# The joint network's first chunk: its tanh rows by DMA transposes instead of TensorE, and an earlier place for the next chunk's x tiles

## The chip, the cores and the metric

The kernel runs on one core of a Trainium2 chip. The metric is the device time of one execution in microseconds; lower is better. The engines are named as in the profile: PE (TensorE, with PEld for its weight loads), DVE (VectorE), ACT (ScalarE), POOL (GpSimd) and SP (SyncE), which here only issues DMAs.

## The reference, cut to what matters

The kernel computes the forward and the backward pass of a small transducer ("joint") network in bfloat16:

```python
B, T, D, K, U = 2, 16000, 256, 3, 8
h  = gelu(conv3(x, w1))[:, ::2]            # (B, 8000, D)
f  = gelu(conv3(h, w2))[:, ::2]            # (B, 4000, D)
fe = f @ w_f                               # (B, 4000, D)
ge = g @ w_g                               # (B, U, D)
j  = tanh(fe[:, :, None] + ge[:, None])    # (B, 4000, U, D)
out = j @ w_o                              # (B, 4000, U, D)
# and the gradients of x, w1, w2, g, w_f, w_g, w_o for a given grad_out
```

Two matmuls read j with different sides on the partitions. `out` takes j as it is made (D on partitions, time along the row). The gradient of w_o is the sum over time of j times grad_out, so it needs j with time on the partitions: the "tanh rows".

## The kernel before, in words

**Tiling.** The 4000 time steps of each of the two sequences are cut into 8 chunks of 512 (the last has 416), so there are G = 16 chunks, n = 0 to 15. In a chunk the 8 values of u are taken in 4 pairs, `up` = 0 to 3.

**Main work of a pair** (`joint_units`, L602): for each of its two u, `gj` (L518) makes the square of tanh JSQ on ACT (L523), multiplies GOT (grad_out, transposed as it is loaded) with w_o on PE (L529) and forms NGZ on DVE (L531); POOL adds NGZ up (L550). Then `o_block` (L618) makes four blocks of the output, 128 time steps each: four matmuls JT x WO (L623), an eviction on ACT (L625), and one store for the pair (L652). Between these blocks stand the matmuls of `gwo` (L664, L672), which add the tanh rows JR times GO (grad_out in natural layout) of the pair before into the PSUM bank GWO_ps. Ahead of the output blocks, `ahead()` (L800) starts the tanh of the next pair (L312, ACT, into JT) and calls `load_jr` (L552) for it.

**Tanh rows.** `load_jr` takes a JR tile (3 buffers). In chunks 1 to 15 it fills it with four DMA transposes on SP's queue (L563), one for each of two u and two halves of D, 128 x 512 each, from JT. In chunk 0 it returns at L558 with the tile empty, and `joint_units` calls `jr_block` (L597) for each of the four blocks: four PE transposes into a PSUM tile (L380) and one copy of 128 x 512 by DVE (L382).

**Fill.** While the pairs of chunk n run, PE also makes the two convolutions and FE of chunk n + 1 (`conv_units` L246, `conv2_units` L279, `fe_units` L302, gelu on ACT and DVE at L197 and L199) and, from n = 1 on, the backward convolutions of chunk n - 1. `weave` (L681) takes `ratio` units of this fill for each unit of the main work. Chunk 1's first tanh needs chunk 1's FE.

**Queues and order.** The program's text does not fix the order on an engine: a scheduler places the instructions when the kernel is built, each engine then runs its own list strictly in order, and tiles from small pools (x tiles XC: 6 buffers, GOT: 6, GO: 3, PSUM tiles: 7) are waited for when they come free. SP's queue carries the loads of XC (L134, L138; transposing), GOT (L144; transposing), GO (L152) and the JR transposes (L563). Before the first chunk, L749 to L755 load GOT for u = 0 and 1, GO of pair 0, GOT for u = 2 and 3, and then the four x tiles of chunk 1. In each pair, one x tile of chunk n + 2, one GO and two GOT are loaded (L790 to L798).

Of the kernel before, what the change touches and what calls it, by code (L numbers as in the profile page):

```python
# [32 lines left out]
def kernel(  # L33
# [27 lines left out]
    G = len(chunks)  # L61
    xq = x.rearrange("b (q four) d -> b four q d", four=4)

    def geom(n):
        b, ci = chunks[n]
        c0 = ci * CW
        return b, ci, c0, min(CW, MQ - c0)

    def blocks(w):
        return [(o, min(P, w - o)) for o in range(0, w, P)]  # L70
# [59 lines left out]
    def load_x(n, c):  # L130
        b, ci, c0, W = geom(n)
        t = xcp.tile([P, KT, CW + 16], BF16, name="XC")
        if c == 3 and ci > 0:
            nc.sync.dma_start_transpose(out=t[:, :, 0:W + 16], in_=xq[b, c, c0 - 16:c0 + W, :])  # L134
        else:
            if c == 3:
                nc.vector.memset(t[:, :, 0:16], 0.0)
            nc.sync.dma_start_transpose(out=t[:, :, 16:16 + W], in_=xq[b, c, c0:c0 + W, :])  # L138
        S[n]["X", c] = t

    def load_got(n, u):
        b, ci, c0, W = geom(n)
        t = gotp.tile([P, KT, CW], BF16, name="GOT")
        nc.sync.dma_start_transpose(out=t[:, :, 0:W], in_=grad_out[b, c0:c0 + W, u, :])  # L144
        S[n]["GOT", u] = t

    def load_go(n, up):
        b, ci, c0, W = geom(n)
        t = gop.tile([P, 4, 2 * V], BF16, name="GO")
        nfull = W // P  # L150
        src = grad_out[b, c0:c0 + nfull * P, 2 * up:2 * up + 2, :]
        nc.sync.dma_start(out=t[:, 0:nfull, :], in_=src.rearrange("(tb p) u v -> p tb (u v)", p=P))  # L152
        S[n]["GO", up] = t
        r = W - nfull * P
        if r and up % 2 == 0:
            t = tailp.tile([P, V], BF16, name="GOs")
            for i in range(4):
                nc.sync.dma_start(out=t[i * r:(i + 1) * r, :], in_=grad_out[b, c0 + nfull * P:c0 + W, 2 * up + i, :])
            S[n]["GOs", up // 2] = t
# [358 lines left out]
    def gj(n, u):  # L518
        b, ci, c0, W = geom(n)
        st = S[n]  # L520
        JT, GOT = st["JT", u], st["GOT", u]
        JSQ = jsp.tile([P, KT, CW], BF16, name="JSQ")
        nc.scalar.activation(out=JSQ[:, :, :W], in_=JT[:, :, :W], func=ACT.Square)  # L523
        NGZ = ngzp.tile([P, KT, CW], BF16, name="NGZ")
        st["NGZ", u] = NGZ
        for mt in range(KT):
            ps = ps_f32()
            for kt in range(KT):
                nc.tensor.matmul(ps[:, :W], lhsT=WOT[:, kt, mt * P:(mt + 1) * P], rhs=GOT[:, kt, :W],  # L529
                                 start=(kt == 0), stop=(kt == KT - 1))  # L530
            nc.vector.scalar_tensor_tensor(out=NGZ[:, mt, :W], in0=JSQ[:, mt, :W], scalar=1.0, in1=ps[:, :W],  # L531
                                           op0=ALU.subtract, op1=ALU.mult,
                                           accum_out=NGGEc[:, b, mt, u, ci:ci + 1])
            yield
# [17 lines left out]
    def load_jr(n, up):  # L552

        W = geom(n)[3]
        nfull = W // P
        JR = jrp.tile([P, 4, 2, KT, P], BF16, name="JR")
        S[n]["JR", up] = JR
        if n == 0:  # L558
            return
        for j in range(2):  # L560
            JT = S[n]["JT", 2 * up + j]
            for kt in range(KT):
                nc.sync.dma_start_transpose(out=JR[:, 0:nfull, j, kt, :], in_=JT[:, kt, 0:nfull * P])  # L563
# [38 lines left out]
    def joint_units(n, up, ahead):  # L602
        b, ci, c0, W = geom(n)
        st = S[n]
        bl = blocks(W)[:W // P]
        us = (2 * up, 2 * up + 1)
        for u in us:
            yield from gj(n, u)
            ngfe_acc(n, u)
            short_jt(n, u)  # L610
        if n == 0:
            for k in range(len(bl)):
                jr_block(n, up, k)
                yield
        OUT = outp.tile([P, 4, 2 * V], BF16, name="OUT")
        JR = st["JR", up]

        def o_block(k):  # L618
            o, M = bl[k]
            ps = ps_f32()  # L620
            for j, u in enumerate(us):
                for kt in range(KT):
                    nc.tensor.matmul(ps[:M, j * V:(j + 1) * V], lhsT=st["JT", u][:, kt, o:o + M], rhs=WO[:, kt, :],  # L623
                                     start=(kt == 0), stop=(kt == KT - 1))
            nc.scalar.copy(out=OUT[:M, k, :], in_=ps[:M, :])  # L625

        ahead()
        pend = prev_gwo[0]
        o_block(0)
        yield  # L630
        o_block(1)
        yield
        if pend is not None:
            gwo(*pend, 0)
        yield
        if pend is not None:
            gwo(*pend, 1)
        yield
        for k in range(2, len(bl)):
            o_block(k)  # L640
            yield
            if pend is not None:
                gwo(*pend, k)
        yield
        if pend is not None:
            gwo_rest(*pend, len(bl))
        yield
        if W % P and up % 2:
            yield from short_block(n, up // 2)
        prev_gwo[0] = (n, up)  # L650
        nfull = W // P
        nc.gpsimd.dma_start(out=out_0[b, c0:c0 + nfull * P, us[0]:us[1] + 1, :].rearrange("(tb p) u v -> p tb (u v)", p=P),  # L652
                            in_=OUT[:, 0:nfull, :])
# [94 lines left out]

    for i in range(2):  # L749
        load_got(*order[i])  # L750
    load_go(*orderp[0])
    for i in range(2, 4):
        load_got(*order[i])
    for c in (1, 0, 3, 2):
        load_x(1, c)  # L755
    for _ in chain(warm(16), small_units(), conv_units(0), transposed_units(), warm(4), conv2_units(0), warm(16), fe_units(0)):
        pass
    for u in range(2):
# [3 lines left out]
    for n in range(G):  # L762
        back, fwd = n > 0, n + 1 < G
        conv = conv_units(n + 1) if fwd else iter(())
        parts = []
        if back:
            for (o, M) in blocks(window(n - 1)[1] - window(n - 1)[0]):
                load_x5(n - 1, o, M)
            d1, e, gwf = d1_units(n - 1), e_units(n - 1), gwf_units(n - 1)
            nfn = (len(blocks(geom(n - 1)[3])) + 1) // 2  # L770
            d5, gw2 = d5_units(n - 1), gw2_units(n - 1)
            nhg = len(blocks(geom(n - 1)[3]))
            parts += [islice(conv, 2), islice(d1, 1), islice(conv, 1), d1, conv,
                      islice(gwf, 1), islice(d5, 1), islice(gwf, nfn - 1), islice(d5, 1), islice(gw2, 1),
                      islice(d5, 1), islice(gw2, 1), d5, islice(gw2, nhg - 2), gwf, gw2]
        else:
            parts += [conv, iter([None] * 3)]
        if fwd:
            parts.append(conv2_units(n + 1))
        if back:  # L780
            parts.append(islice(e, 6))
        else:
            parts.append(iter([None] * 3))
        if fwd:
            parts.append(fe_units(n + 1))
        if back:
            parts.append(e)
        fill = chain(*parts)
        ratio = (0.85 if n > 0 else 0.28) if n + 1 < G else 0.72
        for up in range(U // 2):  # L790
            step = n * (U // 2) + up
            if n + 2 < G:
                load_x(n + 2, (1, 0, 3, 2)[up])
            if step + 1 < len(orderp):
                load_go(*orderp[step + 1])
            for i in range(2):
                if 2 * step + 4 + i < len(order):
                    load_got(*order[2 * step + 4 + i])  # L798

            def ahead():  # L800
                for i in range(2):
                    if 2 * step + 2 + i < len(order):
                        tanh(*order[2 * step + 2 + i])
                if step + 1 < len(orderp):
                    load_jr(*orderp[step + 1])

            weave(joint_units(n, up, ahead), fill, ratio)
            if up == U // 2 - 1:
                for _ in fill:
                    pump(2)  # L810
                pump(len(later) + len(lazy))
                lazy_on[0] = False
    n = G - 1
# [44 lines left out]
    t_ = gel3.tile([P, 512], BF16, name="g_sq", tag="g_sq")  # L858
    nc.scalar.activation(out=t_[:], in_=GWG_ps[:], func=ACT.Copy, scale=-1.0)
    nc.sync.dma_start(out=out_6.rearrange("(dt p) n -> p dt n", p=P), in_=t_[:].rearrange("p (k n) -> p k n", k=KT))  # L860


# [1 line left out]
_INS = ['x', 'w1', 'w2', 'g', 'w_f', 'w_g', 'w_o', 'grad_out']  # L864
_OUTS = [((2, 4000, 8, 256), 'bfloat16'), ((2, 16000, 256), 'bfloat16'), ((3, 256, 256), 'bfloat16'), ((3, 256, 256), 'bfloat16'), ((2, 8, 256), 'bfloat16'), ((256, 256), 'bfloat16'), ((256, 256), 'bfloat16'), ((256, 256), 'bfloat16')]
# [25 lines left out]
```

## Time and profile before

| | us |
|---|---|
| median of the 3 runs | 872.27 |
| the three runs | 867.04, 872.27, 877.83 |
| the profiled execution | 865.23 |
| its span in the profile | 863.5 |
| PE, DVE, ACT, POOL busy in it | 830.8, 603.8, 685.7, 410.6 |
| DMA queue q1 (SP), share of 16 engines | 76.4% |

The span is counted from the first to the last thing that the profile holds; the time of the execution has 1.7 us more around it. All times in a trace are counted from the span's start. In the rows of a timeline, the first number is the start, the second the length, "x16" joins that many equal instructions, and the bracket tells how long the engine sat idle before and what ended that. A group row gives busy time and mean length in ns. For SP, a row is the time in which the queue issued the DMA, not that of the transfer.

### The profile page before, as it was taken

Reading aid. Unit: us, or ns where it says so; the run is one execution under the profiler, and the core shown is the slowest. Engines: PE = TensorE matmul, PEld = TensorE weight load, DVE = VectorE, ACT = ScalarE, POOL = GpSimd, SP = SyncE. Lnnn points to the kernel's source line nnn. Section 1 sums busy time; section 2 is a strip of 40 time slices with the busy share of each in tenths; the row PEclk is TensorE's granted clock in tenths of the full one; section 3 lists DMA queues with packets and bytes.
Section 4 is the critical chain, followed back from the end, with each engine's and each line's share of the span. In section 5 each row is a group of like instructions: output and inputs, shape, how many; then the busy total and the mean of one; then the engine's idle time right before and its main releaser. Section 6 shows DMA issues by size and latency. Waiting matters only on the chain.

```text
span 863.5 us, 17775 instructions
## 1 busy us (share of the span) xinstructions
PE 830.8 (96%) x6648; PEld 598.9 (69%) x6648; DVE 603.8 (70%) x1194; ACT 685.7 (79%) x1067; POOL 410.6 (48%) x457
## 2 busy tenths in 40 slices
PE   8878999999999999999999999999999999999997
PEld 4455776767777677777766677776766867777875
DVE  4797949669495784949578495875949579495553
ACT  4889896986969869696996969788696986969534
POOL 1264553544544544555454455453554544455651
PEclk9999999999999999999999999999999999999999
DMA  9998999999999999999899999999999999999942
GB/s 187 211 215 195 189 250 224 224 243 193 258 206 227 226 217 233 212 227 219 211 203 214 234 215 240 227 210 250 177 263 236 205 211 219 219 243 219 215 140 91
DMA packets 382455, 185.66 MB, mean 215 GB/s; under 512 B 330160, under 2 KB 366280, under 8 KB 382368
## 3 DMA queue, kind: packets, MB, share of 16 engines
q1 hardware_dynamic: 362400, 114.35, 76.4%
q0 software_dynamic: 19968, 70.18, 27.9%
q8 instruction: 52, 0.85, 0.4%
q14 instruction: 35, 0.29, 0.1%
HBM read 54.43 MB, written 50.34 MB: 121 GB/s over the span
## 4 chain that ended last, share of the span: by engine, by line
PE 51%; DVE 30%; ACT 13%; issue 3%; DMA 2%; POOL 0%; ACTq 0%; POOLq 0%; DVEq 0%
PE ps L500 7%; PE ps L246 7%; PE GWO_ps L672 7%; PE ps L529 7%; PE ps L478 7%; PE ps L623 6%; DVE NGZ L531 6%; DVE G L199 5%; DVE g_sq L199 5%; DVE g_s L197 5%; DVE GH L369 3%; ACT JSQ L523 3%; ACT JT L312 3%; PE pst L380 3%; PE ps L366 3%
## 5 line engine op out<-in xcount | busy, mean ns | idle before, releaser
L550 POOL TENSOR_TENSOR ACCN<-ACCN,NGZ 128x1024 f32<-128x1024 f32 (+1 forms) x80 | 170.4, 2130 | 126.5 <-DVE NGZ L531 124.0
L531 DVE SCALAR_TENSOR_TENSOR NGZ<-JSQ,ps 128x512 bf16<-128x512 bf16 (+1 forms) x256 | 163.4, 669 | 83.5 <-ACT GX L481 47.7
L523 ACT ACTIVATE JSQ<-JT 128x1024 bf16<-128x1024 bf16 (+1 forms) x128 | 135.3, 1060 | 86.6 <-DVE NGZ L531 86.6
L312 ACT ACTIVATE JT<-FE,GE 128x512 bf16<-128x512 f32 (+1 forms) x256 | 171.0, 736 | 0.1
L625 ACT CAST OUT<-ps 128x512 bf16<-128x512 f32 x248 | 147.7, 614 | 3.8 <-PE ps L623 3.3
L623 PE MATMUL ps<-WO,JT 128*128 128x256 bf16 x992 | 148.1, 272 | 0.9 <-DVE NGZ L531 0.5
L529 PE MATMUL ps<-GOT,WOT 128*128 128x512 bf16 (+1 forms) x512 | 138.4, 374 | 1.7 <-DVE JR L382 1.1
L672 PE MATMUL GWO_ps<-GO,JR 128*128 128x256 bf16 x992 | 139.7, 273 | 0.0
L197 DVE SCALAR_TENSOR_TENSOR g_s<-g_sq,g_x 128x1024 bf16<-128x1024 bf16 (+1 forms) x45 | 74.6, 1657 | 57.1 <-ACT g_sq L197 57.1
L623 PEld LDWEIGHTS <-JT 128*128 128x128 bf16 x992 | 94.4, 98 | 24.9 <-issue 1.4
L672 PEld LDWEIGHTS <-JR 128*128 128x128 bf16 x992 | 95.1, 98 | 18.2 <-issue 1.1
L322 DVE TENSOR_TENSOR ACC<-ACC,ps 128x512 f32<-128x512 f32 x90 | 59.4, 682 | 66.6 <-PE ps L500 62.0
L478 PE MATMUL ps<-W1T,GH 128*128 128x256 bf16 (+2 forms) x768 | 104.2, 273 | 0.0
L500 PE MATMUL ps<-rows,X 128*128 128x256 bf16 (+2 forms) x768 | 94.2, 272 | 8.2 <-DVE rows L382 8.2
L246 PE MATMUL ps<-XC,W 128*128 128x512 bf16 (+1 forms) x384 | 91.1, 374 | 2.5 <-DMA XC<-in_x_dram 2.1
L500 PEld LDWEIGHTS <-X 128*128 128x128 bf16 (+2 forms) x768 | 74.5, 98 | 23.1 <-issue 11.5
L652 POOL DMA_DIRECT2D out_dram<-OUT x64 | 49.6, 775 | 85.2 <-ACT OUT L625 82.8
L481 ACT CAST GX<-ps 128x512 bf16<-128x512 f32 (+2 forms) x128 | 74.4, 592 | 15.0 <-PE ps L478 7.8
L478 PEld LDWEIGHTS <-GH 128*128 128x128 bf16 (+2 forms) x768 | 75.0, 99 | 15.6 <-issue 1.7
L529 PEld LDWEIGHTS <-WOT 128*128 128x128 bf16 x512 | 49.1, 98 | 43.9 <-issue 2.6
L490 POOL DMA_DIRECT2D out_dram<-GX x64 | 35.9, 560 | 87.3 <-ACT GX L481 81.0
L382 ACT COPY rows<-pst 128x1024 bf16<-128x1024 bf16 x64 | 63.0, 1018 | 9.6 <-PE pst L380 9.5
(139 smaller groups left out, 1264.5 us busy)
## 6 DMA issues: line engine op xcount, KB each, us to landing
GO<-in_grad_out_dram SPq DMA_DIRECT2D x56, 512.0 KB, 5.3
out_dram<-OUT POOLq DMA_DIRECT2D x56, 512.0 KB, 5.6
X<-in_x_dram POOLq DMA_DIRECT2D x58, 320.0 KB, 8.0
out_dram<-GX POOLq DMA_DIRECT2D x58, 256.0 KB, 4.1
JR<-JT SPq DMA_TRANSPOSE x240, 5.1
GO<-in_grad_out_dram SPq DMA_DIRECT2D x8, 384.0 KB, 4.1
out_dram<-OUT POOLq DMA_DIRECT2D x8, 384.0 KB, 4.7
GOT<-in_grad_out_dram SPq DMA_TRANSPOSE x128, 4.6
```

The source lines that it names most:

```text
L197: later.popleft()()
L246: nc.tensor.matmul(ps[:, :W], lhsT=W1[:, i, kt, mt * P:(mt + 1) * P], rhs=st["X", c][:, kt, 16 + sh:16 + sh + W], start=(k == 0), stop=(k ...
L312: nc.scalar.activation(out=JT[:, mt, :W], in_=S[n]["FE"][:, mt, :W], func=ACT.Tanh, bias=GE[:, b, mt, u:u + 1], scale=1.0)
L478: nc.tensor.matmul(ps[:Mx, cj * D:(cj + 1) * D], lhsT=GH[:, par, kt, j:j + Mx], rhs=W1T[:, i, kt, :], start=(k == 0), stop=(k == last))
L500: nc.tensor.matmul(ps[:, dt * D:(dt + 1) * D], lhsT=st["X5", o][:M, i + 2 * par, dt * P:(dt + 1) * P], rhs=t[:M, j + 2 * par:j + 2 * par + ...
L523: nc.scalar.activation(out=JSQ[:, :, :W], in_=JT[:, :, :W], func=ACT.Square)
L529: nc.tensor.matmul(ps[:, :W], lhsT=WOT[:, kt, mt * P:(mt + 1) * P], rhs=GOT[:, kt, :W], start=(kt == 0), stop=(kt == KT - 1))
L531: nc.vector.scalar_tensor_tensor(out=NGZ[:, mt, :W], in0=JSQ[:, mt, :W], scalar=1.0, in1=ps[:, :W], op0=ALU.subtract, op1=ALU.mult, accum_ ...
L550: nc.gpsimd.tensor_tensor(out=out, in0=in0, in1=st["NGZ", u][:, :, :W], op=ALU.add)
L623: nc.tensor.matmul(ps[:M, j * V:(j + 1) * V], lhsT=st["JT", u][:, kt, o:o + M], rhs=WO[:, kt, :], start=(kt == 0), stop=(kt == KT - 1))
L625: nc.scalar.copy(out=OUT[:M, k, :], in_=ps[:M, :])
L672: nc.tensor.matmul(GWO_ps[:, dt, :], lhsT=JR[:M, k, j, dt, :], rhs=GO[:M, k, j * V:(j + 1) * V], start=(n_gwo[0] == 0), stop=(n_gwo[0] == ...
```

## The change

1. `load_jr` and `joint_units` treat as special only pair 0 of chunk 0, no longer all of chunk 0. Pairs 1 to 3 of chunk 0 get their tanh rows by four DMA transposes each, as in all later chunks; pair 0 keeps PE transposes and DVE copies.
2. Of the x tiles of chunk 1, c = 1 and c = 0 are loaded before GO of pair 0, and c = 3 and c = 2 after it, ahead of GOT for u = 2 and 3.
3. The number of fill units for each main unit in chunk 0 goes from 0.28 to 0.36. A pair without `jr_block` has four main units less.

```diff
@@ load_jr
-        if n == 0:
+        if (n, up) == (0, 0):
             return
@@ joint_units
-        if n == 0:
+        if (n, up) == (0, 0):
             for k in range(len(bl)):
                 jr_block(n, up, k)
                 yield
@@ before the first chunk
     for i in range(2):
         load_got(*order[i])
+    for c in (1, 0):
+        load_x(1, c)
     load_go(*orderp[0])
+    for c in (3, 2):
+        load_x(1, c)
     for i in range(2, 4):
         load_got(*order[i])
-    for c in (1, 0, 3, 2):
-        load_x(1, c)
@@ the loop over chunks
-        ratio = (0.85 if n > 0 else 0.28) if n + 1 < G else 0.72
+        ratio = (0.85 if n > 0 else 0.36) if n + 1 < G else 0.72
```

The scheduler places the instructions of the changed program anew. On SP, between the x load that stands at 37.40 us in the profile and chunk 1's first JR, the order was: three XC, two GOT, GO, two GOT, GO, two GOT, GO. It is now: four JR of pair 1, three XC, two GOT, GO, four JR of pair 2, two GOT, GO, four JR of pair 3, GO, two GOT. On PE, L302 for chunk 1 came after the last pair's L529; it now comes after 16 GWO matmuls of pair 2 and three GWO matmuls of pair 3, with the last pair's L529 behind its first half. Of chunk 1's x tiles only c = 1 has another place in SP's list: ahead of GO of pair 0 and GOT for u = 2 and 3 instead of behind them.

## The prediction

> **What bounds the kernel now.** I read the page first, then the busy time by stage, then PE's and SyncE's rows in order of time between 26 and 72 us, since the change touches only chunk 0 (n = 0) and the loads just ahead of it.
>
> ```profile
> span 863.5 us, 17775 instructions
> PE 830.8 (96%) x6648; PEld 598.9 (69%) x6648; DVE 603.8 (70%) x1194; ACT 685.7 (79%) x1067; POOL 410.6 (48%) x457
> ```
>
> ```profile
> 39.00:52.00 13.00, 10.91 (x78) 6.68 (x77) 12.24 (x24) 11.61 (x18) 7.21 (x5) 1.00 1.24 214
> 52.00:65.00 13.00, 10.01 (x91) 7.41 (x90) 12.93 (x25) 11.21 (x18) 8.53 (x5) 1.00 0.83 226
> 600.00:653.00 53.00, 51.82 (x418) 37.59 (x416) 37.56 (x72) 43.38 (x67) 25.58 (x27) 1.00 1.17 237
> ```
>
> The second view's columns are PE, PEld, DVE, ACT and POOL busy, the granted clock, the DMA engines' share and GB/s. From chunk 1 on PE is the bound (51.82 of 53 us), so whatever moves the start of chunk 1 moves the end by as much. Chunk 0 is different: PE is idle 2 to 3 us in each 13, and VectorE has no idle time (12.24 and 12.93 of 13). What PE waits for there is the chain that makes chunk 1's FE, and it ends at 63 us:
>
> ```profile
> 58.16 1.91 PE L672 MATMUL GWO_ps<-GO,JR 128*128 128x256 bf16 x16
> 63.04 0.59 PE L302 MATMUL ps<-FT,WF 128*128 128x512 bf16 x2 [2.97 <-DVE FT L197]
> 66.86 1.03 PE L623 MATMUL ps<-WO,JT 128*128 128x256 bf16 x8 [0.34 <-DVE JR L382]
> 69.40 0.59 PE L529 MATMUL ps<-GOT,WOT 128*128 128x512 bf16 x2 [1.07 <-DVE JR L382]
> 70.33 1.02 PE L246 MATMUL ps<-XC,W 128*128 128x512 bf16 x4 [0.34 <-DVE JR L382]
> ```
>
> SyncE's queue (start, length) is what the change loads more:
>
> ```profile
> 37.40 1.25 SPq L134 DMA_TRANSPOSE XC<-in_x_dram  x1
> 38.74 5.19 SPq L138 DMA_TRANSPOSE XC<-in_x_dram  x3
> 44.03 3.23 SPq L144 DMA_TRANSPOSE GOT<-in_grad_out_dram  x2
> 47.35 0.53 SPq L152 DMA_DIRECT2D GO<-in_grad_out_dram  x1
> 48.53 4.19 SPq L144 DMA_TRANSPOSE GOT<-in_grad_out_dram  x2
> 56.63 0.38 SPq L152 DMA_DIRECT2D GO<-in_grad_out_dram  x1
> 57.50 2.57 SPq L144 DMA_TRANSPOSE GOT<-in_grad_out_dram  x2
> 60.16 0.53 SPq L152 DMA_DIRECT2D GO<-in_grad_out_dram  x1
> 65.04 5.33 SPq L563 DMA_TRANSPOSE JR<-JT  x4
> 70.46 1.82 SPq L144 DMA_TRANSPOSE GOT<-in_grad_out_dram  x1
> ```
>
> It is nearly full until 52 us, has 52.7 to 56.6 and 60.7 to 65 free, and a step of four JR transposes takes 70.46 - 65.04 = 5.42 us, 1.355 each.
>
> **What the change removes.** 3 pairs x 4 blocks = 12 groups of four PE transposes (48 in all) and 12 copies JR<-pst. Back to back, 16 transposes take 63.47 to 64.36 us, 0.89, so PE loses 3 x 0.89 = 2.7 us. VectorE's row is:
>
> ```profile
> L382 DVE COPY JR<-pst 128x512 bf16<-128x512 bf16 x16 | 6.0, 412 | 1.5 <-PE pst L380 1.5
> ```
>
> 12 x 412 ns = 4.9 us, in a stretch where VectorE is full and makes FT. If nothing else were late, FT and with it FE would come up to 4.9 us sooner, at about 58.1. It is "up to", because part of the copies' time lay under POOL's sums: the product at 56.28 took 2.56 us where its like take 0.68, ending with POOL's sum. The bounds are -4.9 and 0.
>
> **What it adds.** 12 DMA transposes on SyncE's queue, 12 x 1.355 = 16.3 us, into a stretch (38.7 to 65 us) with 8 us free. The order of the built program shows where: after the load of XC that stands at 37.40 come the four of pair 1, three XC loads, two GOT, one GO, the four of pair 2, two GOT, one GO, the four of pair 3. And on PE it puts 16 GWO matmuls of pair 2 and then three GWO matmuls of pair 3 ahead of L302, the matmul of chunk 1's FE. PE takes its instructions in order, so FE now waits for three of pair 3's transposes, where it waited for FT. That is the wait that takes the old one's place. Behind it on PE stand FE, the last pair's L529 and L623 and all of chunk 1; behind it on ScalarE stand FE's copies and the tanh of chunk 1's first pair.
>
> When do these three land? SyncE starts at 38.74. Before the third transpose of pair 3 go 10 JR, 3 XC and 4 GOT steps of 1.35 us (57.50 to 60.16 gives 1.33 for a GOT) and two GO of 0.62: 17 x 1.35 + 1.24 = 24.2, so it is issued at 62.9. From issue to landing the page has 5.1 us for a JR: 68.0. Low: 1.30 a step (three JR at 102.19 to 106.10) and 3.3 us to landing (the median at 65 to 85 us): 62.1 + 3.3 = 65.4. High: 1.72 for each XC and GOT, as at 38.74 to 47.35: 65.5 + 5.1 = 70.6. I take 68.0, made of the median rows. None of these steps waits longer for its source: the tanh rows of pair 3 are ready some 4 us before SyncE gets to them at 60.2 (ScalarE has them at 56.07 today), the buffers likewise. L302 starts at 68.0 against 63.04: **+5.0** (+2.4 to +7.6).
>
> After L302 PE has 8 matmuls L529 more (the last pair's, in front of FE before): 8 x 0.217 (starts of pairs are 0.43 apart) = +1.74; 16 transposes less, -0.89; 3 GWO less, -0.33: **+0.5**. The three waits for "DVE JR" in the lines above go: 0.34 + 1.07 + 0.34 = **-1.75**. ScalarE has to make the last pair's two JSQ between the two FE copies instead of before them, 2 x 0.99 = 2.0 (the rows of two at 51.14 and 29.46 took 2.00 and 1.99); chunk 1's first JSQ and the PSUM evictions come that much later, partly under PE's conv work: 0 to 2.0, I take the middle, **+1.0**.
>
> The clock: PE would stand nearly idle from about 55 to 68 us, with 2 us of GWO work in between. Before, its longest wait here is 2.97 us, at clock 1.00. After the last matmul of the run (ends 859.0) the granted clock (third column from the end) falls to a half at about 860.5:
>
> ```profile
> 859.60:860.10 0.50, 0.00 (x0) 0.00 (x0) 0.00 (x0) 0.04 (x1) 0.00 (x0) 1.00 0.00 0
> 860.10:860.60 0.50, 0.00 (x0) 0.00 (x0) 0.00 (x0) 0.00 (x0) 0.00 (x0) 0.86 0.02 6
> 860.60:861.10 0.50, 0.00 (x0) 0.00 (x0) 0.00 (x0) 0.00 (x0) 0.00 (x0) 0.50 0.83 254
> ```
>
> and at the start the warming matmuls of L711 run 0.427 us apart from 1.66 to 7.16 us, twice the later 0.217: up to 5.5 us at half speed, which costs 2.75. Bounds 0 and 2.75; I take the middle, **+1.4**. The Trainium skill's page "TensorE: Matmul & The Clock Gate" (What's actually happening) says that an idle window of about 3.4 us halves PE's clock and about 3.4 us of work restores it. By that rule, as an estimate, the stall costs 1.7 us instead of 1.4 and the sum below is 6.5 instead of 6.2; the fall at the end agrees in kind though it came 1.5 us after the last matmul, and no row of this run shows a return in mid-kernel.
>
> **The load order** I cost at nothing. In the built order only x tile c=1 of chunk 1 moves, three places ahead of one GO and two GOT; the tile that PE waits for (c=3, issued at 26.12, used at 31.17 after a wait of 2.15 us) has the same place, behind as many transfers, since its buffers and the queue's order hold it there. The GO and GOT passed come 1.3 us later and are needed at 39 us. Bounds: -0.4 (two L529 that now stand behind conv no longer fill) to +0.4. The new ratio only sets how the conv work is spread in chunk 0 and is in the order read above.
>
> **The sum** is 5.0 + 0.5 - 1.75 + 1.0 + 1.4 = **+6.2 us**, with the parts' ends +1.2 (2.4 + 0.5 - 1.75 + 0 + 0) and +11.1 (7.6 + 0.5 - 1.75 + 2.0 + 2.75). The profiled execution took 865.2 us (span 863.5), so it would take 871.4; the median of the three runs shown is 872.27, 7 us above, and I put the time on that: 872.27 + 6.2 = 878.5, in its own range 873.5 to 883.4.
>
> **Rivals.**
> 1. Faster: pair 3's rows land before FT is made, and the freed VectorE decides. FE starts at 58.1: -4.9 + 0.5 - 1.75 + 1.0 = -5.2 us, 867.1. For it: VectorE is full and its copies stand in the chain of waits. Against it: it is true only if the third transpose of pair 3 lands by 58.1, and the queue's steps would then have to average 0.8 us, where no transpose in the trace is issued in under 1.18. Between 58 and 63 us the gain shrinks to nothing. Chance 0.18, as PE may be less bound to these rows than the order says.
> 2. The DMA engines become the bound. A JR transpose moves half of what a GOT or XC does; queue q1's 76.4% of 863.5 us over 240/2 + 128 + 64 = 312 of the larger (its plain loads counted in, so at most) is 2.1 us each, 1.06 for a JR, 12.7 for twelve. If the engines, at 1.17 in steady work, can't take it in, all of it is passed on: +12.7, 885.0. For it: 1.24 at 39 to 52 us. Against it: 0.83 in the next 13, and PE's waits from 72 to 850 us name no DMA. Chance 0.17.
> 3. No change: the stall in chunk 0 is made up, because chunk 1's first pair is bound by ScalarE either way; 872.3, within 2 us. PE's idle time from 72 to 850 us is 778 - 764 = 14 us, in small gaps behind DVE that a late start doesn't shorten. Chance 0.1.
>
> **Chances.** Forecast 0.55, the rivals 0.18, 0.17 and 0.1. The range reaches from rival 1's time, 867, to a little past rival 2's, 887; the three runs of before differ by 10.8 us themselves. 2% is 17.4 us, about what a measurement of this kernel can tell from no change. Every case lies inside it; only the high end of the forecast together with rival 2 (11.1 + 12.7) goes past: slower 0.05, faster 0.01, within 0.94.
>
> **What would show it.** PE idle in front of GWO_ps<-GO,JR (L672), put down to DMA JR, for some us before 68 us; L302 of chunk 1 at 65 to 71 us instead of 63.04; VectorE with idle time in 39 to 65 us; SyncE without a gap from 38 to 65 us; a granted clock under 1.00 just after; twelve JR copies and 48 transposes gone; the conv wait at 31.17 still there. The steady stage should keep its 51.8 of 53 us. I am wrong if L302 starts before 63 us, or if PE waits for transfers in chunks 1 and 2.

## The result and the profile after

| | before | after |
|---|---|---|
| median of 22 runs each, us | 867.43 | 874.08 |
| lowest and highest | 864.45, 878.59 | 870.43, 891.03 |
| ratio | | 1.0073, 95% interval 1.0055 to 1.0091 |
| span of the profiled execution | 863.5 | 872.1 |
| its own time | 865.23 | 873.9 |

The changed kernel is slower by 0.73% (867.43 x 0.0073 = 6.3 us, 4.8 to 7.9 by the interval), well inside 2%. The prediction's difference was +6.2. Its absolute time, 878.5, is 4.4 us too high, since it stood on the median of three runs (872.27), which 22 runs put at 867.43. Ratios in this document leave disturbed executions out, so the median of all runs of a kernel can stand higher than its ratio says, and the profiles of rows_only and best_warm fell in such executions, so that only the ratios of these two are used.

From the page after, the busy times and the group of the weight-gradient matmuls:

```profile
PE 834.8 (96%) x6600; PEld 597.9 (69%) x6600; DVE 601.2 (69%) x1182; ACT 684.9 (79%) x1067; POOL 408.2 (47%) x457
...
L672 PE MATMUL GWO_ps<-GO,JR 128*128 128x256 bf16 x992 | 142.1, 275 | 7.9 <-DMA JR<-JT 7.7
```

48 PE instructions and 12 of VectorE's are gone, as written. Yet PE is busy 4.0 us longer (834.8 against 830.8): the clock, below. A wait for a DMA of tanh rows (7.7 us, none before) has appeared in front of L672.

By stage (PE, PEld, DVE, ACT, POOL busy, granted clock, DMA share, GB/s), first the one row of before that the prediction doesn't show, then the rows after:

```profile
65.00:78.00 13.00, 10.72 (x64) 6.03 (x63) 9.41 (x20) 11.21 (x21) 8.27 (x9) 1.00 0.78 199
```

```profile
39.00:52.00 13.00, 11.36 (x74) 6.89 (x73) 10.52 (x16) 13.00 (x21) 5.00 (x4) 1.00 0.92 178
52.00:65.00 13.00, 8.18 (x47) 4.94 (x45) 12.83 (x21) 8.49 (x13) 7.31 (x6) 0.75 0.98 212
65.00:78.00 13.00, 8.77 (x35) 4.18 (x36) 3.94 (x10) 5.77 (x9) 3.47 (x2) 0.59 0.73 182
600.00:653.00 53.00, 51.82 (x413) 37.41 (x411) 37.46 (x71) 43.62 (x68) 25.61 (x27) 1.00 1.07 227
```

The steady stage keeps its 51.82 of 53 us. The loss shows between 52 and 78 us, where PE is idle 9 us (5.3 before) and the clock is 0.75 and 0.59 (1.00 before); from 65 us on VectorE and ScalarE have little to do either. PE's rows in order of time:

```profile
57.51 0.27 PE L672 MATMUL GWO_ps<-GO,JR 128*128 128x256 bf16 x1
59.55 1.40 PE L672 MATMUL GWO_ps<-GO,JR 128*128 128x256 bf16 x3 [1.76 <-DMA JR<-JT]
61.12 2.95 PE L672 MATMUL GWO_ps<-GO,JR 128*128 128x256 bf16 x13 [0.18 <-DMA JR<-JT]
67.33 0.39 PE L672 MATMUL GWO_ps<-GO,JR 128*128 128x256 bf16 x1 [3.25 <-DMA JR<-JT]
69.35 0.39 PE L672 MATMUL GWO_ps<-GO,JR 128*128 128x256 bf16 x1 [1.63 <-DMA JR<-JT]
70.01 0.40 PE L672 MATMUL GWO_ps<-GO,JR 128*128 128x256 bf16 x1 [0.27 <-DMA JR<-JT]
70.20 1.06 PE L302 MATMUL ps<-FT,WF 128*128 128x512 bf16 x2
71.06 2.77 PE L529 MATMUL ps<-GOT,WOT 128*128 128x512 bf16 x6
73.62 1.06 PE L302 MATMUL ps<-FT,WF 128*128 128x512 bf16 x2
```

Three matmuls of 0.4 us each, one per transpose of pair 3, hold L302 until 70.20 (63.04 before), and each waits for its own rows. FT had been ready since 63.85 (62.99 before). Two L302 now take 1.06 us where they took 0.59, and the rows keep that pace until 75.5 us: half clock, in the midst of work. SP's queue:

```profile
38.99 6.52 SPq L563 DMA_TRANSPOSE JR<-JT  x4
45.60 3.95 SPq L138 DMA_TRANSPOSE XC<-in_x_dram  x3
49.64 2.60 SPq L144 DMA_TRANSPOSE GOT<-in_grad_out_dram  x2
52.33 0.53 SPq L152 DMA_DIRECT2D GO<-in_grad_out_dram  x1
52.95 6.21 SPq L563 DMA_TRANSPOSE JR<-JT  x4
59.26 2.61 SPq L144 DMA_TRANSPOSE GOT<-in_grad_out_dram  x2
61.96 0.53 SPq L152 DMA_DIRECT2D GO<-in_grad_out_dram  x1
62.59 6.96 SPq L563 DMA_TRANSPOSE JR<-JT  x4
```

The queue has no gap from 38.99 to 69.55. The order is the forecast one, the steps are longer: 6.2 to 7.0 us for four JR, against the 5.42 the prediction took.

### The profile page after: what moved, and what is told of

It reads as the page before. It is cut to its first block, busy times and chain, and to the rows that moved or that the text cites. A ratio compares the mean times of both kernels' runs of the same rounds, so it can differ in the third digit from the quotient of the medians.

```text
span 872.1 us, 17699 instructions
## 1 busy us (share of the span) xinstructions
PE 834.8 (96%) x6600; PEld 597.9 (69%) x6600; DVE 601.2 (69%) x1182; ACT 684.9 (79%) x1067; POOL 408.2 (47%) x457
## 4 chain that ended last, share of the span: by engine, by line
PE 49%; DVE 29%; ACT 16%; DMA 3%; issue 2%; POOL 0%; SPq 0%; ACTq 0%; POOLq 0%; DVEq 0%
PE ps L500 7%; PE ps L478 7%; PE ps L529 7%; PE GWO_ps L672 6%; DVE NGZ L531 6%; PE ps L623 6%; PE ps L246 6%; DVE G L199 5%; DVE g_sq L199 5%; DVE g_s L197 5%; ACT JT L312 4%; DVE GH L369 3%; ACT JSQ L523 3%; ACT g_sq L197 3%; PE pst L380 3%
## 5 line engine op out<-in xcount | busy, mean ns | idle before, releaser
L672 PE MATMUL GWO_ps<-GO,JR 128*128 128x256 bf16 x992 | 142.1, 275 | 7.9 <-DMA JR<-JT 7.7
L529 PE MATMUL ps<-GOT,WOT 128*128 128x512 bf16 (+1 forms) x512 | 140.5, 379 | 0.7 <-ACT OUT L625 0.7
L672 PEld LDWEIGHTS <-JR 128*128 128x128 bf16 x992 | 95.7, 98 | 29.0 <-DMA JR<-JT 10.4
L246 PE MATMUL ps<-XC,W 128*128 128x512 bf16 (+1 forms) x384 | 91.7, 376 | 2.8 <-DMA XC<-in_x_dram 2.7
L529 PEld LDWEIGHTS <-WOT 128*128 128x128 bf16 x512 | 49.6, 99 | 44.4 <-issue 4.0
```

The lines of the kernel that those rows point to most:

```text
L246: nc.tensor.matmul(ps[:, :W], lhsT=W1[:, i, kt, mt * P:(mt + 1) * P], rhs=st["X", c][:, kt, 16 + sh:16 + sh + W], start=(k == 0), stop=(k ...
L672: nc.tensor.matmul(GWO_ps[:, dt, :], lhsT=JR[:M, k, j, dt, :], rhs=GO[:M, k, j * V:(j + 1) * V], start=(n_gwo[0] == 0), stop=(n_gwo[0] == ...
```

## The experiments

Single spans differ by several us for reasons that lie outside the disturbed stretch. Ahead of it is the wait for x tile c=3 at 31 us: the last group of chunk 1's first convolution begins anywhere from 36.00 to 40.71 us. Behind it, from the first L406 to the end, most profiles take 773 to 777 us, but pair3_pe takes 783 (5.8 us of waits for JR in later chunks) and more_dma 789. So in each profile I count from the last group of chunk 1's first convolution (the last L246 row ahead of L302), with three marks: FT's start on VectorE, L302, and the first matmul of the gradient of w_f (L406) behind it, which PE reaches after all of the disturbed stretch. The expectations count from the second group, two groups earlier; where a group runs at half clock that origin is less steady.

| kernel | last group at | FT | L302 | first L406 | ratio to before, 95% |
|---|---|---|---|---|---|
| before | 37.72 | +24.58 | +25.32 | +52.20 | 1 |
| after | 38.28 | +24.89 | +31.92 | +59.32 | 1.0073 (1.0055 to 1.0091) |
| loads_only | 40.71 | +24.58 | +25.32 | +52.20 | 1.0006 (0.9967 to 1.0045) |
| rows_only | | | | | 1.0087 (1.0041 to 1.0133) |
| fe_first | 39.26 | +24.88 | +25.62 | +54.74 | 1.0036 (0.9992 to 1.0080) |
| pair3_pe | 37.58 | +24.88 | +25.99 | +53.53 | 1.0037 (0.9996 to 1.0078) |
| x_late | 36.00 | +24.89 | +27.17 | +53.62 | 1.0039 (0.9997 to 1.0082) |
| fe_first_warm | 38.48 | +24.83 | +25.56 | +52.48 | 1.0003 (0.9989 to 1.0018) |
| no_pool | 38.15 | +20.70 | +21.44 | +50.70 | 1.0009 (0.9973 to 1.0044) |
| more_dma | 38.27 | +25.08 | +40.37 | +68.28 | 1.0284 (1.0202 to 1.0366) |

In the diffs, `behind(a, b)` puts instruction a after b in the list of its engine, without a wait.

**One half of the change at a time.** loads_only is the kernel before with the new order of the first loads, rows_only the changed kernel with the old one:

```diff
+    for c in (1, 0):
+        load_x(1, c)
     load_go(*orderp[0])
-    for i in range(2, 4):
-        load_got(*order[i])
-    for c in (1, 0, 3, 2):
+    for c in (3, 2):
         load_x(1, c)
+    for i in range(2, 4):
+        load_got(*order[i])
```

> The kernel before with the new order of the loads alone (part 2 of the change). On SP only the x tile c=1 of chunk 1 moves, the order on the compute engines is that of before. My theory (the loss is made by the tanh rows on SP's queue): no change, within 0.2%, and the conv of chunk 1 still waits for the x tile c=3 until about 31.2 us. Rival (the new load order delays GO and GOT of the first pairs and makes part of the loss): 0.2 to 0.4% slower.

> The changed kernel with the old order of the loads (parts 1 and 3 alone). The order on PE is that of the changed kernel. My theory: all of the change's loss, +0.6 to +0.9% against before, with chunk 1's FE (L302) at about 70 us. Rival (the loads share in it): +0.3 to +0.5%.

loads_only: +52.20, the same to the hundredth as before, and a ratio around 1. rows_only: slower, with an interval that takes in that of the whole change. The cost lies in the rows with the new fill ratio, which rows_only has as well. By itself the ratio costs nothing that is seen (fe_first_warm, below); whether it shares in the new order on PE no run tells. What the loads do alone can't be told from 0, give or take 0.4%. The marks say nothing on the loads, since they count from behind the wait for x tile c=3. In loads_only that wait lasted 3.52 us, until 32.58 instead of the expected 31.2; but with the same order of loads it lasted 1.48 us in pair3_pe and 3.59 in fe_first.

**The order on PE.** fe_first keeps the transposes, but places the weight-gradient matmuls of pairs 2 and 3 behind chunk 1's FE in PE's list:

```diff
@@ fe_units
-                nc.tensor.matmul(ps[:, :W], lhsT=WF[:, kt, mt * P:(mt + 1) * P], rhs=S[n]["FT"][:, kt, :W],
+                m = nc.tensor.matmul(ps[:, :W], lhsT=WF[:, kt, mt * P:(mt + 1) * P], rhs=S[n]["FT"][:, kt, :W],
...
+                mark["FE", n] = m
@@ gwo
+                if n == 0 and up >= 2:
+                    behind(m, mark["FE", 1])
```

> The changed kernel with one edit: on PE the GWO matmuls of pairs 2 and 3 of chunk 0 are queued behind the matmuls of chunk 1's FE; all transfers stay, in the same order on SP. My theory (FE waits in PE's list for pair 3's rows): FE starts when FT is made, at about 64 us, and the time is 6 us less than that of the changed kernel, -0.1 to +0.2% against before. Rival A (the freed VectorE time is worth something once the wait is gone): FT comes at 59 to 61 us and the kernel is 0.3 to 0.5% faster than before. Rival B (the DMA engines are the limit, so what isn't waited for here is waited for in chunk 1): still +0.5 to +0.8%.

PE in this kernel (L308 is the old L302, L536 the old L529):

```profile
64.88 1.01 PE L308 MATMUL ps<-FT,WF 128*128 128x512 bf16 x2 [6.11 <-DVE FT L203]
65.68 2.76 PE L536 MATMUL ps<-GOT,WOT 128*128 128x512 bf16 x6
```

The wait for rows is gone, L302 follows FT, and the mark at L406 falls from +59.32 to +54.74: 4.6 of the 7.1 us came from these matmuls standing ahead of FE. The ratio falls to 1.0036, 3.2 us less where 6 were expected, its interval still meeting that of the change, so that the ratio alone doesn't rule out rival B. FT came no sooner (+24.88), against rival A. But PE now idles 6.11 us in one piece, waiting for FT, and comes back at half clock (1.01 us for two matmuls): 2.5 us are left.

**The clock.** fe_first_warm puts 24 matmuls on a resident weight tile, whose result is not read, into that stall:

```diff
@@ fe_units
+        if n == 1:
+            hold = ps_f32()
+            for k in range(24):
+                m = nc.tensor.matmul(hold[:].rearrange("p (a b) -> p a b", a=KT), lhsT=W1[:, 0, 0, 0:P], rhs=W1[:, 0, :, :], start=True, stop=True)
+                behind(m, mark["WARM"] if k else mark["GWO"])
+                mark["WARM"] = m
```

> The kernel with the FE matmul ahead of the weight-gradient matmuls of pairs 2 and 3, and 24 matmuls of 128x512 on a resident weight tile put into the stall ahead of L302 (their result is not read). Theory of the clock: the granted clock in 52 to 78 us stays above 0.93 instead of 0.80, L302 begins at the same place (+30 from the second conv group), and the first L406 comes at +56.5 to +57 instead of +59.3; the whole 1.5 to 2.7 us below the same kernel without them (871.9), about 869 to 870. Rival (the clock costs nothing since ScalarE and VectorE set the pace after L302): L406 at +59 and 872. Rival (matmuls in the stall delay L302): L302 at +32 or later.

Its PE rows, and its stages:

```profile
57.81 5.34 PE L306 MATMUL ps<-W 128*128 128x512 bf16 x24
64.04 0.59 PE L314 MATMUL ps<-FT,WF 128*128 128x512 bf16 x2 [0.89 <-DVE FT L203]
64.47 1.46 PE L544 MATMUL ps<-GOT,WOT 128*128 128x512 bf16 x6
```

```profile
52.00:65.00 13.00, 10.36 (x61) 5.77 (x60) 12.86 (x20) 9.85 (x15) 7.46 (x6) 1.00 0.97 216
65.00:78.00 13.00, 13.00 (x84) 8.02 (x82) 7.31 (x21) 12.87 (x22) 10.15 (x9) 1.00 1.18 215
```

The clock stays at 1.00, L302 is where it was, six L529 take 1.46 us instead of 2.76, and L406 comes 2.3 us sooner (+52.48). The whole is back at the time of before, 1.0003, with an interval clear of the change's. So the clock is worth 2.3 us by the mark. (From the second group the mark is +57.7, not the expected +57; that group itself ran at half clock, 2.72 us.) Taken away in this order, the three parts add up: 7.12 us lost = 4.58 for the order on PE + 2.26 for the clock + 0.28 left. This kernel also keeps all twelve transposes and the new fill ratio. Its ratio, 0.9989 to 1.0018, thus says that the two together cost less than 0.2% once FE doesn't wait for the rows, which leaves no room for rival B's 0.5%.

**The place on SP's queue.** x_late leaves PE's order as the change has it and queues three x tiles of chunks 2 and 3 behind pair 3's transposes:

```diff
@@ load_x
+        if (n, c) in ((2, 2), (3, 1), (3, 0)):
+            behind(d, mark["JR", 0, 3])
```

> The changed kernel with one difference: the loads of the later x tiles (chunk 2 c=2, chunk 3 c=1 and c=0) are queued on SP behind the four transposes of pair 3's tanh rows instead of ahead of pair 2's and 3's. All times from the start of chunk 1's second conv group (L246). Theory (SP issues in order, pair 3's rows stand behind 6 to 8 us of other issues): pair 3's rows are issued about 4 us sooner, L302 begins at +31 to +33 instead of +36.0, the first L406 at +58.5 to +60.5 instead of +63.4, and the whole is 870 to 871 us beside 867.4 of before and 874.1 of after. Rival (DMA engines are what is late): the three x tiles then only move behind and the rows still land late, L302 at +35 to +36 and 873 to 875 us. Rival (freed VectorE work decides): no difference, since FT isn't touched: +36.

SP's third step of four, and what PE waited for:

```profile
56.74 5.11 SPq L572 DMA_TRANSPOSE JR<-JT  x4
```

```profile
62.04 0.28 PE L681 MATMUL GWO_ps<-GO,JR 128*128 128x256 bf16 x1 [4.79 <-DMA JR<-JT]
62.52 0.86 PE L681 MATMUL GWO_ps<-GO,JR 128*128 128x256 bf16 x2 [0.20 <-DMA JR<-JT]
63.17 1.06 PE L311 MATMUL ps<-FT,WF 128*128 128x512 bf16 x2
```

From the last group, pair 3's transposes begin at +20.7 instead of +24.3, and L302 comes at +27.17 instead of +31.92. The mark at L406 falls by 5.7 us, by more than was expected, with no change of PE's list: what lay ahead in the queue made the rows late. The ratio, 1.0039, is the 871 us expected, though its interval still meets that of the change.

**Pair 3 alone.** pair3_pe gives pair 3 back to PE and VectorE and leaves pairs 1 and 2 with the transposes:

```diff
-        if (n, up) == (0, 0):
+        if (n, up) in ((0, 0), (0, 3)):
```

> The changed kernel with pair 3 of chunk 0 back on PE transposes and VectorE copies, pairs 1 and 2 by DMA. SP has four steps less before chunk 1, and on PE only the GWO of pair 2 stands ahead of chunk 1's FE; its rows land at about 62 us. My theory: FE starts at about 64 us and the time is that of before, -0.1 to +0.3%. Rival (every DMA transpose in chunk 0 costs its share of engine time): two thirds of the loss stay, +0.5%.

L302 at +25.99, L406 at +53.53: of the 7.1 us lost, 5.8 come with pair 3's rows. That is what my theory says, by the mark. The ratio, 1.0037, lies just above the expected +0.3%, and its interval rules out neither the theory nor the rival's +0.5%; the 5.8 us of JR waits in later chunks stand in this profile.

**The DMA engines.** more_dma is the changed kernel with the stores of three OUT tiles made three times:

```diff
+        if n == 0 and up < 3:
+            for i in range(2):
+                nc.gpsimd.dma_start(out=out_0[1, i * CW:(i + 1) * CW, us[0]:us[1] + 1, :].rearrange("(tb p) u v -> p tb (u v)", p=P),
+                                    in_=OUT[:, 0:nfull, :])
```

> The changed kernel with each of the first three OUT tiles of chunk 0 (512 KB each) stored twice more through GpSimd's queue, to places that later chunks overwrite: 3 MB more in the stretch from 40 to 70 us. Theory (the SP queue's order sets when rows arrive, the engines have room): the DMA share in 52 to 65 us rises, L302 begins within 1.5 us of +36.0 from the second conv group, and the whole within 2 us of 874.1. Rival (the DMA engines are the bound there): 3 MB at some 200 GB/s are 15 us of the engines, L302 is 5 us or more later and the whole 879 or more.

My theory missed here. L302 came 8.5 us later (+40.37), the rival's case. SP's rows tell how:

```profile
43.52 9.35 SPq L138 DMA_TRANSPOSE XC<-in_x_dram  x3
52.96 5.09 SPq L144 DMA_TRANSPOSE GOT<-in_grad_out_dram  x2
...
59.50 5.33 SPq L563 DMA_TRANSPOSE JR<-JT  x4
64.92 6.00 SPq L144 DMA_TRANSPOSE GOT<-in_grad_out_dram  x2
...
71.64 5.56 SPq L563 DMA_TRANSPOSE JR<-JT  x4
```

Three XC took 9.35 us to issue (3.95 after), two GOT 5.09 and 6.00 (2.60 and 2.61). The four JR did not take longer: 5.33 and 5.56 us for pairs 2 and 3, beside 6.21 and 6.96 after. The time from issue to landing tells the same, by its medians between 38 and 80 us: 2.9 us for JR (3.1 after), but 5.3 for XC (3.9) and 7.2 for GOT (3.5). So the loads from DRAM got slower in this profile, the queue passed it on, and pair 3's rows began at +33.4 instead of +24.3. Queue and engines are thus not two separate causes. The change itself adds 12 transposes of 128 KB, half of these 3 MB; how much of its longer steps is the engines' load no run tells apart. The ratio in the table stands on two executions, and the profiled one lost 14 us more behind the mark (789 us to the end, 774.5 after), so it doesn't measure this stretch.

**Why the freed VectorE bought nothing.** FT starts at +24.6 to +25.1 in eight of the nine profiles, with the 12 copies or without. In the changed kernel VectorE's long rows there are:

```profile
47.04 2.30 DVE L197 TENSOR_TENSOR HT<-g_s,g_x 128x1024 bf16<-128x1024 bf16 x1
...
50.48 2.35 DVE L199 TENSOR_SCALAR g_sq<-g_sq 128x1024 bf16<-128x1024 bf16 x1
...
58.77 2.21 DVE L197 SCALAR_TENSOR_TENSOR g_s<-g_sq,g_x 128x1024 bf16<-128x1024 bf16 x1
61.01 2.23 DVE L199 TENSOR_SCALAR g_sq<-g_sq 128x1024 bf16<-128x1024 bf16 x1
63.17 0.68 DVE L197 TENSOR_TENSOR FT<-g_s,g_x 128x1024 bf16<-128x1024 bf16 x1
```

Each lies beside one of GpSimd's sums, which begin at 46.68, 50.10 and 57.78 us (there two in a row, to 62.95). Each is 1.0 to 1.9 us longer than its like elsewhere (0.69, 0.42, 1.22, 0.42): 6.3 us together. no_pool takes fe_first and leaves those sums out:

```diff
@@ ngfe_acc
-        if u == 0:
+        if u == 0 or (n == 0 and 2 <= u < U - 1):
             return
```

> The kernel with the FE matmul ahead of the weight-gradient matmuls of pairs 2 and 3, and with GpSimd's sums over u = 2 to 6 of chunk 0 left out, so that the gradient sum of that chunk lacks those terms. Theory (VectorE's rows wait for GpSimd's sums, 6.3 us of it between 45 and 63 us, which is why the removed copies brought no sooner FT): VectorE's rows of 2.2 to 2.4 us there fall to 0.4 to 1.2, FT is done at +25 to +27 from the second conv group instead of +30, L302 right behind it, and the whole is 3 to 5 us below 871.9. Rival (FT is held by the order of VectorE's list and by ScalarE's Derivative inputs, not by GpSimd): VectorE's rows shorten but FT stays within 1 us of +30 and the whole within 1.5 us of 871.9.

```profile
46.91 0.69 DVE L203 TENSOR_TENSOR HT<-g_s,g_x 128x1024 bf16<-128x1024 bf16 x1
...
48.73 0.42 DVE L205 TENSOR_SCALAR g_sq<-g_sq 128x1024 bf16<-128x1024 bf16 x1
...
55.53 1.22 DVE L203 SCALAR_TENSOR_TENSOR g_s<-g_sq,g_x 128x1024 bf16<-128x1024 bf16 x1
56.78 0.43 DVE L205 TENSOR_SCALAR g_sq<-g_sq 128x1024 bf16<-128x1024 bf16 x1
58.85 0.69 DVE L203 TENSOR_TENSOR FT<-g_s,g_x 128x1024 bf16<-128x1024 bf16 x1 [1.64 <-ACT g_s L203]
```

All four rows fall to their own length, and FT comes 4.2 us sooner (+20.70): the theory holds for FT, and ScalarE is next (1.64 us). It holds in part for the whole: L406 comes 4.0 us sooner, the ratio falls by 0.0027, 2.3 us where 3 to 5 were expected, and the two intervals overlap. The Trainium skill's page "SBUF — State Buffer" (section "SBUF: two separate sides") says that VectorE and GpSimd share a pair of ports, which one of them holds for a whole instruction when VectorE's operation has two inputs in SBUF or runs in a two-port mode. The rows agree: 0.69 became 2.30 beside a GpSimd sum of 2.12 us.

**Better versions.** Three kernels went for a time below that of before. x_first is the kernel before with chunk 0's later grad_out loads behind chunk 1's x tiles on SP, best_warm has the same order in fe_first_warm, and best_sum also moves the sums of u = 2 to 5 to VectorE:

```diff
@@ load_got
+        if n == 0 and u >= 4:
+            behind(d, mark["X1"])
@@ load_go
+        if n == 0 and up >= 1:
+            behind(d, mark["X1"])
@@ ngfe_acc, in best_sum alone
-        nc.gpsimd.tensor_tensor(out=out, in0=in0, in1=st["NGZ", u][:, :, :W], op=ALU.add)
+        eng = nc.vector if n == 0 and 2 <= u < U - 2 else nc.gpsimd
+        eng.tensor_tensor(out=out, in0=in0, in1=st["NGZ", u][:, :, :W], op=ALU.add)
```

> The kernel before with one difference: on SP's queue chunk 0's later grad_out tiles (the transposes of u from 4 on, and the plain loads of pairs 1 and 2) are issued behind chunk 1's four x tiles, so that the x tile c=3, which conv group 2 of chunk 1 waits for, stands three places sooner. Theory (that tile's place on SP's queue sets when PE goes on at 33 us): the wait of 1.4 to 3.0 us there goes, and the last conv group of chunk 1 begins at 35 to 36.5 us instead of 37.7; the whole is 1 to 3 us below 867.4, if the grad_out tiles aren't late next. Rival (the gain is taken back by a grad_out tile that comes late): the last group sooner, but VectorE's NGZ or PE's GO waits for a DMA behind it and the whole is within 1 us of 867.4.

> The changed kernel with the FE matmul ahead of the weight-gradient matmuls of pairs 2 and 3, the 24 matmuls in the stall ahead of L302, and chunk 1's x tiles ahead of grad_out on SP as in the kernel of that name. From the last group of chunk 1's first conv: FT at +24.9, L302 at +25.5, first L406 at +52.5, as without the load order (52.48). Theory: the load order adds 1 to 3 us of gain, so 864 to 866 us. Rival (no gain from the loads): 867.

> The same as the kernel with all three mends, and with GpSimd's sums over u = 2 to 5 of chunk 0 put on VectorE. Theory (VectorE waited for GpSimd's sums, 6.3 us of it ahead of FT, and the transposes gave VectorE 4.9 us of room): the four long rows fall to 0.4 to 1.2 us, four sums of some 1.1 to 2.2 us are added to VectorE, and FT comes at +19 to +25 instead of +24.9 from the last group of chunk 1's first conv; the whole is 0 to 4 us below the same kernel with GpSimd's sums. Rival (a sum costs VectorE as much as waiting for GpSimd's did): no difference, within 1 us.

x_first: 866.55 us beside 867.75, ratio 0.9979 (0.9949 to 1.0010). PE's wait for the x tile (2.15 us before) is gone, the last group begins at 36.33 instead of 37.72, and L406 follows at +52.28, so 1.3 us of it are kept that far. In the whole they can't be told from none. best_warm: 0.9981 (0.9937 to 1.0025), no better than x_first. best_sum: 1.0005 (0.9961 to 1.0048). A sum takes VectorE 1.22 us and GpSimd 2.12, and FT came at +24.1, 0.8 us sooner than the +24.9 usual here, but L302 at +25.5, no sooner than in fe_first_warm (+25.56). FT was ready at 59.58 us, and the 24 matmuls of the filled stall ran on to 60.47: now they held FE up. L406 came only at +58.7, after two more waits of 2.71 and 1.89 us for JR. The expected gain is not seen. The ratio is 0.0024 above best_warm's, with intervals that overlap, so a loss isn't shown either. None of the three is shown to beat the kernel before.

## Why the prediction was right, step by step

The sign and the mechanism were right. Some terms missed and offset each other, so that it is partly luck how close +6.2 came to the measured 6.3. By the marks, the stretch to L302 lost 6.6 us (31.92 - 25.32) where +5.0 was predicted. The stretch from L302 to L406 lost 0.5 (27.40 after, 26.88 before) where 0.5 - 1.75 + 1.0 + 1.4 = +1.15 was; by the runs its terms are 0.5 - 2.3 + 0 + 2.3. The profiled spans differ by 8.6: 7.1 here, 0.6 from the x tile's wait ahead of it, and about 1.0 behind it, which single profiles spread by anyway.

- **The wait for pair 3's rows (+5.0, ends 2.4 to 7.6).** Right in kind, shown by fe_first and x_late, and 1.6 us small. The failed piece is the 1.355 us of a step. The third transpose of pair 3 was issued at 65.22, not 62.9: (65.22 - 38.99 - 1.25 for two GO) / 17 = 1.47 a step. Most steps took 1.2 to 1.3 us, and one in each four JR 2.3 to 2.6. It had landed by 70.0, 4.8 after issue, near the 5.1 taken.
- **Work moved behind L302 (+0.5) and three VectorE waits gone (-1.75).** The work is as counted: between L302 and L406 the traces have 8 L529 more, 16 transposes and 3 GWO less. The waits are a little small. After the change PE has no wait at all from 70.20 us to L406, so the one for NGZ went too, which the prediction left out:

```profile
65.92 0.60 PE L623 MATMUL ps<-WO,JT 128*128 128x256 bf16 x4 [0.53 <-DVE NGZ L531]
```

1.75 + 0.53 = 2.28 us are gone, and the two terms come to -1.8 instead of -1.25.
- **The clock (+1.4, ends 0 to 2.75).** Too small: 2.26 us by fe_first against fe_first_warm, which agrees with the 0.5 + 1.8 = 2.3 that the stretch from L302 to L406 needs. The clock fell at 58.47 us, 0.7 us after a short matmul, and came back at 75.53, after 5.5 us of nearly unbroken work from 70.0, as at the kernel's start (5.5 us). The upper end was the nearer row. The 5.5 us are no fixed price: in x_late the clock was back at 65.70 us, 3.2 after the work became unbroken at 62.52. The estimate by the Trainium skill's page "TensorE: Matmul & The Clock Gate" (What's actually happening), 1.7, is too low here, since that page has about 3.4 us of work to the return and this trace 5.5.
- **ScalarE's two JSQ between the FE copies (+1.0).** Wrong: 0.

```profile
71.36 0.58 ACT L304 COPY FE<-ps 128x512 f32<-128x512 f32 x1 [7.84 <-PE ps L302]
71.84 2.00 ACT L523 ACTIVATE JSQ<-JT 128x1024 bf16<-128x1024 bf16 x2
74.71 0.58 ACT L304 COPY FE<-ps 128x512 f32<-128x512 f32 x1 [0.87 <-PE ps L302]
```

The second copy of FE found ScalarE free for 0.87 us and waited for PE, which stood in six L529 at half clock. The JSQ had cover, and PE has no wait behind L302 that a late ScalarE could have made.
- **The load order (0).** Not contradicted: loads_only's ratio is 1.0006, with an interval far wider than the 0.4 us of the bounds.
- **VectorE's 4.9 us (bounds -4.9 and 0).** The bounds were right, and the value is 0: FT came 0.3 us later. The doubt, that part of the copies' time lay under GpSimd's sums, was the cause. The lengthened rows hold 6.3 us after and 3.8 before, where three rows took 2.23, 1.35 and 2.56 us against 1.22, 0.42 and 0.68:

```profile
44.41 2.23 DVE L197 SCALAR_TENSOR_TENSOR g_s<-g_sq,g_x 128x1024 bf16<-128x1024 bf16 x1
...
47.57 1.35 DVE L199 TENSOR_SCALAR G<-g_s 128x1024 bf16<-128x1024 bf16 x1
...
56.28 2.56 DVE L199 TENSOR_TENSOR g_sq<-g_sq,HT 128x1024 bf16<-128x1024 bf16 x1
```

So half of the room went into waiting for GpSimd, and VectorE idles 1.7 us longer in 39 to 52 us.
- **Rival 1 (faster)** fails twice: rows landed at 70, not by 58.1, and with that wait taken away (fe_first) L302 came at +25.6, no sooner than before. **Rival 2 (engines)** is wrong in size (+12.7), and fe_first_warm, with all twelve transposes in place, is as fast as before. Its resource is real all the same: in more_dma 3 MB more are paid for. **Rival 3 (made up later)** fails: the ratio's interval leaves 1 out.

What stays open: how the longer SP steps divide between the queue's own pace and the load of the DMA engines, why one issue in each four JR of the change took twice the usual time, and why the mark of no_pool is not seen in full in its whole time.

## What to carry to other kernels

A step moved from busy engines to a DMA queue is paid where the first reader of its result stands in an in-order list: look up what waits behind that reader, and move the reader behind the critical matmul before the transfer is blamed. Freed time on a full engine bought nothing here, while another engine's instructions lengthened its rows; look for rows well above the usual length of their kind. A stall of 6 us on PE cost its length and then some 2 us more at half clock, so a stall that cannot go can be worth filling, as long as the filler ends before the result that is waited for (in best_sum it didn't).

## What the hardware showed that I had not expected

- With 3 MB more of stores, transposing loads from DRAM took longer both to issue and to land, and transposes from SBUF to SBUF did not: single issues of XC and GOT took up to 4.35 us (at most 1.26 after, between 38 and 80 us), those of JR 1.2 to 1.4. This is one profile, and single issues of GOT of 5.3 us in the kernel before (at 74.03) and 8.1 in loads_only (at 78.22) stand there without the stores.
- The granted clock fell in mid-kernel within about 0.7 us of PE's last short matmul (57.78 to 58.47 us). In the 3 us ahead PE had worked only 0.7. Matmuls issued 3 us in a row (61.12 to 64.07) did not bring it back; 5.5 us did in this profile, and 3.2 in x_late.
- The stretches at half clock are whole multiples of 3.41 us in four profiles. The times of fall and return follow from the mean granted clock of half-microsecond slices (0.97 in 58.0 to 58.5 us is a fall at 58.47): 58.47 to 75.53 us after, 59.90 to 70.14 in fe_first, 58.30 to 65.12 in no_pool and 62.29 to 65.70 in x_late, which are 5, 3, 2 and 1 times 3.41. If the clock changes on such a grid, the cost of a stall depends on where on it the work begins again; no run moves one stall along it.
- A sum of 128x1024 in f32 takes GpSimd 2.1 us and VectorE 1.22, and a VectorE row of 0.42 us took 2.35 while GpSimd made such a sum.
